# Moving the first row maxima, the spills and the loads of a float32 attention and gated-FFN kernel, with new round orders

## The chip, the cores and the metric

The kernel runs on one core of a Trainium2 chip. The metric is the device time of one execution in microseconds (us), the median over several executions. One more execution is taken with the hardware profiler; its trace is what the views below show.

## The reference

For x of 2048 tokens by 448 features the reference computes an attention block with 16 heads of 28 features, a gated feed-forward block with 1792 hidden features, and mixes the two by a sigmoid gate per token:

```
qkv = x @ wqkv                       # 448 -> 3 x 16 heads x 28
p   = softmax(q k^T / sqrt(28))      # per head, 2048 x 2048
a   = (p v).reshape(S, 448) @ wo
h   = relu(x @ W_gate) * (x @ W_up)  # 448 -> 1792
b   = h @ W_down                     # 1792 -> 448
g   = sigmoid((x * gate_w).sum(-1))
out = g * a + (1 - g) * b
```

All of it is float32.

## The kernel before, in words

**Precision.** A float32 operand is split into a high and a low float32r part, high on ScalarE (`act_high`), low as operand minus high on VectorE (`low`) or on GpSimd (`pool_low`). A product over 448 features takes eleven matmuls (the list `TERMS`): 3 1/2 chunks of 128 features, high by high, high by low and low by high, some of them packed in one matmul.

**First phase (L511 to L606).** The program loads x in four blocks of 512 tokens (`X[tb]`, two parts each), projects part of q and k (`qk`, twelve units), writes them to HBM as `qk_d`, then projects v (`vproj`, sixteen units). The last nineteen of these units stand in the list `mixed`, counted by `n`: n = 0 to 2 are q and k units, n = 3 to 18 the v units, eleven matmuls each. At given values of n the loop also issues loads (`load_k`, `load_q`, `load_w`), splits of weights, and the spills of X to HBM (`spill_x`, table `spills`; part `(tb, r)` is written to `x_d`). From unit `first` on it strews `smax` among the matmuls of a unit: two matmuls of a head's q with its k (`sm`) into a pair of PSUM banks and one VectorE maximum over 1024 values (L259). `MAXIMA` of these are done in the first phase. When all of head 0 are done (20 of them), `smax_end` transposes them on TensorE (`mt`), and two small DMAs of `mh` (L272) write them as two more rows into the tile of q (`Q0`), so that later score matmuls subtract them. EARLY puts the first eight score units of head 0 (`s`) among the last v units. The scores of token block j = 3 (`s_0_3`, `s_2_3` and so on) do not use the `mh` rows; `s_0_0` is the first that does.

**Rounds.** After that come 32 rounds, two for each head (a round is one half of the keys). Each is a string, R0 to R31, that gives the order of the work, a letter for each step: `s` a score unit (two matmuls, one ScalarE evacuation), `m` an `smax` of a later head, `x` one matmul of a projection that is spread over the rounds (first the rest of q and k, 176 matmuls, L669; then the units of gate and up, 22 matmuls each, L661), `b`, `A` running minima and the row correction on VectorE for the chunks that go uncorrected ("raw"), `g` a subtraction on GpSimd (L340), `e`, `E` exponentials on ScalarE over 1024 or 2048 columns, `P`, `Q` the two halves of probabilities times v (32 matmuls of 32 columns each, `po`, L720), `n` `smax_end`, `w` the split of a gate/up weight, and `N`, `c`, `f`, `D` small steps. The order of instructions on every engine is the order of this text: no scheduler changes it. An engine that waits holds back all that stands behind it in its queue.

X[0] is a single pair of tiles. When the last unit of a token block has used a chunk of it, `next_x` (L656) has SyncE load the next block's chunk from `x_d`; the next unit starts with the same chunk nine matmuls later. At the start of an even round SyncE gets the loads of k, and at its ninth `s` those of q, of the head after next.

**Last phase (L899 on).** What is left of gate and up is done between the down projections (`down`, L955). Four output projections (`wout`, L914) follow for each block of tokens; `split_o` (L903 to L907) splits the normalised attention output into `on0`, `on1`, in two halves of 1024 columns: the high part on ScalarE, the low part on GpSimd.

**Queues.** Loads and most stores are issued by SyncE in the order of the program; the stores of the first phase (`qk_d`, `v_d`, `x_d`) by GpSimd.

Of the kernel before, what the change touches and what calls it, by code (L numbers as in the profile page):

```python
# [72 lines left out]
R12 = "sxxsxxgxxbsxwxbwsbxxxsxxxsxxxssxxAxxswsxgExxmxwmsxxxmxxxsmxsgxxmxmxxEsbxsgxxsEbebPAmmeQ"

R13 = "sxxmsbsxxgxxxsxxsxxxbbxsxxxsxsxAsmnxgsxxxxsxmEsxxxexxmxmxxxsmxxgmxxxEmxNcsgxxsxbxsebbAePfeQ"

R14 = "mxsxxsssxxxxbbxxxbsxxxxsxxxsgsxxxxsxxAsmsxxsgxmxxxesmgxemxexxmsexexsbxPebgesemxmbxxAxQ"

R15 = "ssxsgxxsgxbxbxbxxxAgxsxxxsxxxsxsxsxsxxmexNxxxmxsmnxsxxsmeemxxxexxxxxmssxxcxsPxbbbeAegmefmxxeQ"

R16 = "smsxxbxgsxsbxxbxsxxexxsgxxxxxAsxxxsxxsmxsxexmxsmxexxmxsxxggEmxxxmsexxmxxxssxbesbbPeAQ"

R17 = "mxsmnxsggxsxxsxxxxbxxbbAxesxxxxssxxsxxxsxsmxxxsxxemxexmxsxxmxxsxxmxxexxNgmxgcEssbxxbsePebAfQ"

R18 = "smxxgsbsxxbxxgxxsxxxxbxesxxAsxesxxgxsxxxxxxmxxsmxxsmgxsxxsmsxeexxmmesePbsexxmexxxbsbAQ"

R19 = "ssxxsNxbsxxxbxxxxxgxsxgsbxAxxxssxxssxxxgmxxsxmsxmnxxsmxxxmxxmEsexbcxxgxxxsesEPxbxbAefemxmxQ"

R20 = "smgsxxsbxxxgsxxexbxsxxxbmxxsxxsAsxsxxxxxssmxxxgsxmesxmxexmxxxxmxmeEgxxxxssexxsbPebQbA"

R21 = "smsxxsxbxbxsxxxsxgbxxsAxxxgsxssxxxxmsxxxsmsnxxsxmmxxesxebxNxxmxxsxbxxgsxxxxbcgmxxxeAmePEefeQ"

R22 = "sxmsxxsxxbxggsbxxsxxxxbsxxxsAssxxxxmxsxxgsxsEmgxmxxsxmExxxxmxxsemxbsPbxeemsxexxxbxQA"

R23 = "sNmxsxxsxbxsgxxgxxbsxxxxexxbxAsxxssxxmxxxnsxsxxgxsmsxxmxemsxExmcxxxxsxsbxbsbPmxegeexAxxexfmQ"

R24 = "gsmsxxsxsbbxxExxxxxsbgxxmxAgxxxxsxssxxsxsxxxxmxsxmxsxsxmxxxmxExsxbssbPgExxbAemxmeQx"

R25 = "smsxsxbbxsxxbsxnxxsxxsssxxxgAxxsgexxmmNxcsgxexxxmxgsxsxxxmsExxxbxmxsxxxExxmxbsebefAPQxxmxxx"

R26 = "smsxxxsbxxxbsxxxsbxxsxxsgmsxsxgsxxAsxsxmxsmgmmexexxgsExbxxmxxxsxxxxsPbbEexexAxxxxxmQ"

R27 = "smsxxbsxxxxxsxbxsNxbxnsxxgxxsgssxxxxAxsxmexsxmxxcxsxmxgfxsxmxxxmegsxxexbsexxxsxExmPebbAmxexQ"

R28 = "smxmsxxxgxssxxxxxxxbexsxbsxbxxxssxsAxxsgxmxxxsxmsxmxxsxmmxexgmgxExexsxexxxsxsbbbxeexxxxPQA"

R29 = "sxxxxgssbngxbsxbAxxxxExxxxxxsxxsxxxxxssgsxsxxsxxsxNsxxxxxsxxxEcsxgxExbebsxxxxbexfAxxxPQxx"
# [24 lines left out]
def gated_mix_kernel(ctx, tc, x, wq, wo, wgu, wd, out):  # L132
# [43 lines left out]
    def pool_low(dst, src, high):  # L176
        nc.gpsimd.tensor_tensor(dst, src, f32(high), op=OP.subtract)
# [39 lines left out]
    def load_k(h):  # L217
        a = rows_kq(h)[0]
        k = qk_d[a:a + DH].rearrange("d r t -> (d r) t")
        for a in (0, 2 * DH):  # L220
            nc.sync.dma_start(f32(K[h % 3])[a:a + 2 * DH], k)
# [174 lines left out]
    with tc.tile_pool(name="qkv", bufs=1) as pa:  # L396
        W = pa.tile([P, 7, VO + VC], F32R, name="W")

        def load_w(c):
            c0, c1 = c * 2 * GD, (c + 1) * 2 * GD if c < G + 1 else 2 * D + VC  # L400
            wr = pa.tile([P, 4, 2 * GD + 2], F32, name=f"wr_{c0}", tag="wr", bufs=2)[:, :, :c1 - c0]
            if c > 0:
                nc.sync.dma_start(wr, wq[:, :, c0:c1])
# [162 lines left out]
        mixed += [(vproj, tb, t) for tb in range(NB - 1, -1, -1) for t in range(4)]
        spills = {2 + 2 * k: (NB - 1 - k // 2, k % 2) for k in range(2 * NB)}
        m, first, ahead = 0, 4, MAXIMA
        for n, (f, *a) in enumerate(mixed):
# [12 lines left out]
            if n == 8:  # L582
                split_w(*w3, pool_low)
            if n == 10:
                QS.append(last_q("Q2"))
                for i, j in ((GD, 12), (GD + 12, 4)):
                    nc.sync.dma_start(f32(QS[2])[i:i + j].rearrange("p j t -> p (j t)"), Q[1][GD + 2:GD + 2 + j].bitcast(F32))
# [463 lines left out]
```

## Time and profile before

| | |
|---|---|
| median of 3 runs | 1205.58 us (1205.16 to 1208.12) |
| profiled execution | 1207.77 us |
| its span in the trace | 1206.0 us |
| TensorE busy | 1184.7 us (98%) |
| VectorE, ScalarE, GpSimd busy | 75%, 73%, 62% |
| first phase and round 0 | 0 to 128.98 us |
| rounds 1 to 31 | 128.98 to 1015.33 us |
| last phase | 1015.33 to 1206.0 us |

A group of instructions in the profile reads: line, engine, operation, output<-inputs, shapes, count | busy us, mean ns of one | idle time just before, and what ended it. PE is TensorE, PEld its weight loads, DVE VectorE, ACT ScalarE, POOL GpSimd, SP SyncE. Matmuls overlap in the records: the mean of a 512-column matmul is some 400 ns, while starts in a dense stretch are 233 ns apart. A table by stretches gives for each one its length and the busy us (with the count) of each engine, then the granted TensorE clock (1.00 is full), the share of the DMA engines, and GB/s.

### The profile page before, as it was taken

The numbers are of one execution on the slowest core, as the hardware profiler recorded it, in microseconds if no ns is written. First come the engines' busy times: TensorE is split into PE (matmuls) and PEld (weight loads), VectorE is DVE, ScalarE is ACT, GpSimd is POOL, SyncE is SP. The second block draws the span as 40 slices with busy tenths as digits, with TensorE's granted clock in tenths as the row PEclk, the third lists the DMA queues.
The fourth block names the chain that finished last, engine by engine and source line by source line (L and its number), as shares of the span: only waits on it lengthen the run. The fifth ranks groups of instructions, "written<-read, shape, count | busy, mean of one in ns | idle before, by whom it ended". The sixth has DMA issues, their size and how long they took to land.

```text
span 1206.0 us, 16979 instructions
## 1 busy us (share of the span) xinstructions
PE 1184.7 (98%) x6183; PEld 825.1 (68%) x6183; DVE 899.1 (75%) x1171; ACT 881.2 (73%) x1023; POOL 746.6 (62%) x325
## 2 busy tenths in 40 slices
PE   9799999999999999999999999999999999999998
PEld 6688666666666666666666666666666666899998
DVE  5486889888888889889888988888888553643342
ACT  5227888998989888888888888888787887422121
POOL 5232766897889778767776777667666777531020
PEclk9899999999999999999999999999999999999999
DMA  9983574736363654344346344342724335743342
GB/s 304 327 310 117 172 237 160 217 129 185 122 191 124 207 166 141 103 134 118 119 134 215 104 132 125 112 139 98 217 89 139 102 104 160 232 135 112 110 140 81
DMA packets 70656, 188.87 MB, mean 157 GB/s; under 512 B 13946, under 2 KB 20546, under 8 KB 65666
## 3 DMA queue, kind: packets, MB, share of 16 engines
q1 hardware_dynamic: 65756, 167.78, 44.9%
q0 software_dynamic: 4384, 19.53, 4.3%
q8 instruction: 49, 0.80, 0.3%
q10 hardware_dynamic: 432, 0.46, 0.1%
q14 instruction: 35, 0.29, 0.1%
HBM read 126.96 MB, written 60.96 MB: 156 GB/s over the span
## 4 chain that ended last, share of the span: by engine, by line
PE 86%; DMA 4%; DVE 3%; ACT 3%; issue 1%; SPq 1%; POOL 1%; DVEq 0%; ACTq 0%; POOLq 0%
PE gu L661 21%; PE po L720 19%; PE s L361 18%; PE sm L255 10%; PE acc L955 9%; PE qk L669 3%; PE wo L914 3%; PE v L500 3%; DVE r L311 2%; ACT P L367 1%; DMA X<-x_d 1%; DMA Q<-qk_d 1%; DMA or<-o_d 1%; ACT P L365 1%; DMA wor<-wo_d 1%
## 5 line engine op out<-in xcount | busy, mean ns | idle before, releaser
L340 POOL TENSOR_TENSOR P<-P,rm 128x2048 f32<-128x2048 f32 x102 | 470.7, 4632 | 127.8 <-DVE rm L334 111.2
L661 PE MATMUL gu<-X,wg 128*128 128x512 f32 x1232 | 364.3, 397 | 3.2 <-DMA X<-x_d 3.2
L259 DVE TENSOR_REDUCE mx<-sm 128x1 f32<-128x1024 f32 x256 | 306.1, 1217 | 62.5 <-PE sm L255 61.2
L361 PE MATMUL s<-Q,K 128*128 128x512 f32 x1024 | 319.5, 402 | 1.6 <-DVE r L311 0.3
L661 PEld LDWEIGHTS gu<-X,wg 128*128 128x128 f32 x1232 | 229.9, 188 | 73.4 <-issue 8.7
L361 PEld LDWEIGHTS s<-Q,K 128*128 128x128 f32 x1024 | 182.6, 188 | 80.5 <-DVE r L311 12.5
L367 ACT ACTIVATE P<-s 128x1024 f32<-128x1024 f32 x204 | 203.8, 1028 | 45.8 <-PE s L361 43.5
L720 PE MATMUL po<-P,V 128*32 128x512 f32 x1640 | 230.6, 595 | 0.0
L365 ACT ACTIVATE P<-s 128x1024 f32<-128x1024 f32 x206 | 202.4, 1031 | 19.3 <-PE s L361 17.2
L351 ACT ACTIVATE P<-P 128x1024 f32<-128x1024 f32 (+1 forms) x158 | 202.6, 1312 | 0.9 <-POOL P L340 0.5
L255 PE MATMUL sm<-K,Q 128*128 128x512 f32 x520 | 163.8, 401 | 8.3 <-DMA Q<-qk_d 8.1
L311 DVE SCALAR_TENSOR_TENSOR r<-s,r 128x1024 f32<-128x1024 f32 x124 | 151.7, 1223 | 25.7 <-ACT P L367 15.1
L720 PE MATMUL po<-V 128*32 128x512 f32 x408 | 137.1, 595 | 0.0
L720 PEld LDWEIGHTS po<-P,V 128*32 128x32 f32 x1640 | 61.2, 110 | 110.5 <-issue 106.6
L340 POOL TENSOR_TENSOR V<-V,rm 128x2048 f32<-128x2048 f32 x24 | 111.1, 4631 | 31.3 <-DVE rm L334 29.9
L255 PEld LDWEIGHTS sm<-K,Q 128*128 128x128 f32 x520 | 94.3, 189 | 40.9 <-POOL K L578 8.5
L168 ACT ACTIVATE hh<-hr 128x512 fp32r<-128x512 f32 x52 | 32.8, 631 | 114.9 <-PE acc L955 114.9
L174 DVE TENSOR_TENSOR hh<-hr,hh 128x512 fp32r<-128x512 f32 x52 | 48.6, 942 | 80.3 <-ACT hh L168 80.3
L955 PE MATMUL acc<-WD,hh 128*128 128x448 f32 x480 | 100.0, 368 | 0.0
L955 PEld LDWEIGHTS acc<-WD,hh 128*128 128x128 f32 x480 | 91.1, 190 | 7.3
L311 DVE SCALAR_TENSOR_TENSOR r<-s,P 128x1024 f32<-128x1024 f32 x50 | 61.2, 1223 | 26.6 <-ACT P L367 26.1
L326 DVE TRANSPOSE_TENSOR_REDUCE mn<-r 128x32 f32<-128x1024 f32 x63 | 77.8, 1235 | 1.3
(91 smaller groups left out, 1139.2 us busy)
## 6 DMA issues: line engine op xcount, KB each, us to landing
wg<-ws_d SPq DMA_DIRECT2D x42, 896.0 KB
K<-qk_d SPq DMA_DIRECT2D x32, 448.0 KB
Q<-qk_d SPq DMA_DIRECT2D x64, 224.0 KB
X<-x_d SPq DMA_DIRECT2D x56, 256.0 KB
h_d<-h SPq DMA_DIRECT2D x56, 256.0 KB
hr<-h_d SPq DMA_DIRECT2D x52, 256.0 KB
ws_d<-wg SPq DMA_DIRECT2D x14, 896.0 KB
x_d<-X POOLq DMA_DIRECT2D x8, 1024.0 KB, 8.9
```

The costliest lines, as they stand in the source:

```text
L255: nc.tensor.matmul(ps[:, c, :], Q[h][:, u * P:(u + 1) * P], K[h % 3][:, k0:k0 + TB], start=True, stop=True)
L259: nc.vector.tensor_reduce(to, ps, axis=AX.XY, op=OP.max)
L311: nc.vector.scalar_tensor_tensor(r, ps, -1.0, before, op0=OP.mult, op1=OP.min)
L326: nc.vector.tensor_reduce(MN[:, 1:3], R2.pop((v, j)).rearrange("p a (b r) -> p a b r", r=32), axis=AX.X, op=OP.min, apply_transpose=True)
L340: nc.gpsimd.tensor_tensor(QUAD[q], QUAD[q], m, op=OP.subtract)
L351: nc.scalar.activation(q, q, AF.Exp, scale=-SCALE)
L361: nc.tensor.matmul(ps[:, c], K[h % 3][:, k * P:(k + 1) * P], Q[h][:, j * TB:(j + 1) * TB], start=True, stop=True)
L365: nc.scalar.activation(dst, ps, AF.Exp, scale=SCALE)
L367: nc.scalar.activation(dst, ps, AF.Copy, scale=-1.0)
L661: nc.tensor.matmul(ps, WS[i][:, s, a], xf(i // NF, b), start=(n == 0), stop=(n == NT - 1))
L720: nc.tensor.matmul(po[32 * j:32 * j + 32], V[:, h // 4 % 2, k, h % 4], AT.pop((v, k, j)), start=(k == k0), stop=(k == k0 + NK // 2 - 1))
L955: nc.tensor.matmul(ACC[i // NF][t][:, :D], HH[i][:, a, t * P:(t + 1) * P], wd_high_low(f, b), start=(f == 0 and n == 0), stop=(f == NF - 1 ...
```

## The change

It has five parts.

1. `MAXIMA` goes from 36 to 32, and `first` from 4 to 6: the strewn maxima begin two v units later, and four of them move into round 0, whose string now has four `m`.
2. Loads and spills of the first phase: `load_w(3)` goes from ahead of the first head's k and q to behind them (n = 1), k and q of the second head from n = 0 to n = 2, the third weight load from 2 to 3, k of the third head from 6 to 7, the split of that weight from 6 to 10, and the third q tile (`Q2`) from 10 to 13. The eight spills of X, at n = 2, 4, ... 16 before, go to 7, 8, 9, 10, 11, 12, 14, 16, in another order.
3. The strings of all rounds are new. Rounds 19 to 28 now use R11 to R18 over again. A period of eight rounds has 308 `x`, which is fourteen units, one token block. The number of `x`: rounds 0 to 10 as before (44 in rounds 0 to 3, then 40 and 43 in turn); rounds 11 to 28 have 40 (odd) and 37 (even) in place of 43 and 40 (45 in round 28); rounds 29 to 31 have 54 each in place of 50, 47, 50. The sum is 1320 in place of 1364: 59 fewer in rounds 11 to 28, 15 more in rounds 29 to 31, and 44, two units of gate and up, in the last phase.
4. `w` stands in rounds 3 to 10 only (3 to 12 before).
5. For the first token block `split_o` takes the low part on VectorE.

```
-MAXIMA = 36
+MAXIMA = 32
...
-R0 = "xxxsbxxxbxxbxxxxssxxxxsxxAsxxsxxxxsxsxxsxgxxxxxsebxxsxxxxxesxxbxxgbePAeQ"
+R0 = "xxbbsssxxxxsxbxmxxxsxxxxxssxxxxsxAxsxxxxxxmxxxxxgsbsxexxebxxsxxxgmxbxxmePAeQ"
...
-R11 = "xsmxxxgsswxbxwxxxwxxsxxxxxxbsbmsxxsmnsxxssxAxxssxgmxsExxgmmmxxxsEwxxxgNbxxxmxEsbcexexsxbAPfQxx"
+R11 = "sxsxbsxxbgxxxsxxxxsbxxxgsxxsxxssxAxsmgnsxxmsxmNxsxmxEExxxmmsxxxxbxscxxseexxbgefebxxxmAPQ"
...
 ROUNDS = [
     R0, R1, R2, R3, R4, R5, R6, R7,
     R8, R9, R10, R11, R12, R13, R14, R15,
-    R16, R17, R18, R19, R20, R21, R22, R23,
-    R24, R25, R26, R27, R28, R29, R30, R31,
+    R16, R17, R18, R11, R12, R13, R14, R15,
+    R16, R17, R18, R11, R12, R29, R30, R31,
 ]
...
         split_w(*w4)
-        w3 = load_w(3)
         load_k(0)
         load_q(0)
...
-        spills = {2 + 2 * k: (NB - 1 - k // 2, k % 2) for k in range(2 * NB)}
-        m, first, ahead = 0, 4, MAXIMA
+        spills = dict(zip((7, 8, 9, 10, 11, 12, 14, 16), ((3, 0), (2, 0), (2, 1), (1, 0), (3, 1), (1, 1), (0, 0), (0, 1))))
+        m, first, ahead = 0, 6, MAXIMA
         for n, (f, *a) in enumerate(mixed):
             if n == 0:
                 split_w(*w5)
+            if n == 1:
+                w3 = load_w(3)
+            if n == 2:
                 load_k(1)
                 load_q(1)
-            if n == 2:
+            if n == 3:
                 w2 = load_w(2)
...
-            if n == 6:
+            if n == 7:
                 load_k(2)
-                split_w(*w2, pool_low)
             if n == 8:
                 split_w(*w3, pool_low)
             if n == 10:
+                split_w(*w2, pool_low)
+            if n == 13:
                 QS.append(last_q("Q2"))
...
-        pool_low(ON[tb][1][:, c], OR[tb][:, c], ON[tb][0][:, c])
+        (pool_low if tb else low)(ON[tb][1][:, c], OR[tb][:, c], ON[tb][0][:, c])
```

How the instructions stand on two engines at the places that matter. First TensorE, from the first v unit (`v_0`, n = 3) on; `sm` is a maximum's pair of matmuls. Before:

```order
L500 MATMUL v_0_445<-W,X_3_121 128x450 x7
L500 MATMUL v_0_445<-W,X_3_122 128x450 x4
L500 MATMUL v_1_461<-W,X_3_121 128x450 x4
L255 MATMUL sm_468<-K_104,Q_107 128x512 x2
L500 MATMUL v_1_461<-W,X_3_121 128x450 x3
L500 MATMUL v_1_461<-W,X_3_122 128x450
```

and now:

```order
L480 MATMUL v_0_444<-W,X_3_121 128x450 x7
L480 MATMUL v_0_444<-W,X_3_122 128x450 x4
L480 MATMUL v_1_459<-W,X_3_121 128x450 x7
L480 MATMUL v_1_459<-W,X_3_122 128x450 x4
L480 MATMUL v_2_473<-W,X_3_121 128x450 x7
L480 MATMUL v_2_473<-W,X_3_122 128x450 x4
L480 MATMUL v_3_487<-W,X_3_121 128x450 x4
L235 MATMUL sm_494<-K_104,Q_107 128x512 x2
```

The first maximum stands behind 37 matmuls of v in place of 15.

Next SyncE's queue around the first head's k and q (`K_104`, `Q_107`; the second head's are `K_105`, `Q_108`, and `wr` are raw weights). Before:

```order
L403 DMA wr_373<-wq 128x4x224
L221 DMA K_104<-qk_d 56x2048 x2
L230 DMA Q_107<-qk_d 28x2048 x4
L221 DMA K_105<-qk_d 56x2048 x2
L230 DMA Q_108<-qk_d 28x2048 x4
```

and now:

```order
L201 DMA K_104<-qk_d 56x2048 x2
L210 DMA Q_107<-qk_d 28x2048 x4
L383 DMA wr_401<-wq 128x4x224
L201 DMA K_105<-qk_d 56x2048 x2
L210 DMA Q_108<-qk_d 28x2048 x4
```

One weight load moved from ahead of the first q to behind it; the second head's loads still follow directly in this queue. GpSimd's queue, not shown, had the first spill of X among its stores of `qk_d`, and now has it behind them all.

Last, SyncE's queue a little later: the third q tile (`Q_625`, now `Q_684`), the first raw gate/up weights (`wgr`), and the `mh` rows for head 0. Before:

```order
L587 DMA Q_625<-Q_108 12x2048
L587 DMA Q_625<-Q_108 4x2048
L230 DMA Q_625<-qk_d 28x2048 x4
L272 DMA Q_107<-mh_711 1x12x128 x2
L385 DMA wgr_716<-wgu 128x1024
L385 DMA wgr_718<-wgu 128x1024
```

and now:

```order
L570 DMA Q_684<-Q_108 12x2048
L570 DMA Q_684<-Q_108 4x2048
L210 DMA Q_684<-qk_d 28x2048 x4
L365 DMA wgr_691<-wgu 128x1024
L365 DMA wgr_693<-wgu 128x1024
L252 DMA Q_107<-mh_755 1x12x128 x2
```

The `mh` rows now stand behind the two weight loads, and the Q2 loads ahead of both are issued at unit 13 in place of unit 10, in a tile that the spilled part (3, 1) of X leaves free.

More of the change, by code (lines that the diff above doesn't have):

```diff
@@ L73 @@
[L73 to L107, printed above, removed]
@@ L109 @@
-R30 = "sxxsbxssxbxgbgxxsxxsxxAExgxxxxxxsxxssxxxxxxxgsxxsssxxExxxxsExxxxxxxsebsbPxxxbAxeDDxQ"
-R31 = "xsxxxxgxxgxsxbxsbsxxbxxsxxxxAsxxssxxexxxgxxxxxgxxxessxNxxxxxseDxxxxexxxExcxeexPsxDfQ"
+R0 = "xxbbsssxxxxsxbxmxxxsxxxxxssxxxxsxAxsxxxxxxmxxxxxgsbsxexxebxxsxxxgmxbxxmePAeQ"
+R1 = "nsmsxxsgbxbxsxxxgxsxxbxsxxxsxsxxxssAxxmxxsxmsxxmxxxmxgmgExexxxxsxmsxsxxexbsxxbEcxxebmxPeNAfQ"
+R2 = "smsxggbxxsxsxxxsxxbxsbxxxxxssxxxsxxAxggsmxxsxsxExxxmmsxxxmxxxsxsxexbxxxxbxsmebxeeAexPemmQ"
+R3 = "gsmNsxsbxsxwxsbbExxxAxxssmxxwxgxxsxxxxxxxwxmEmcsnxxxgxgxxsxxxsxmxsxxxxmmxfExsxxmxxxssbbsbeePAQw"
@@ new lines @@
+R4 = "smsxxsbxxxwwxxsxxbsgbxxxsxxmsxsxxsxsxsAxmxwxsxxsmsgxgxxxExxbxmxxeexmmxxgxsPbxEesxembwQAx"
+R5 = "NsxxsxxssbgxxxbxxxxwbxxxxsmnxsxsmAsxxswgsxsxxEmxxmxxxxsxxsxmxxEmxxmgsbxexxxxsxxmbegxscbefPeAwwQ"
+R6 = "smsxxxxgxbwssgxxxxxxxsxxxbbxxwemxAssxxxssxsxxmxxsxxsmsxgxexmmsexgbexxxxxsEbemPsewmxwQbxAx"
+R7 = "wssxxbxxsNbxxsbxxxxxgwxsxxxsxmsxsxxxxAsxsgxsxxmnxmxxxesxwsgexmmxxsxbsxxxxcexxsbbAexxmPEgmexfemQw"
+R8 = "smsxgxxswsxxxbxsxwbxbxxsxAxsxxssxgxsmxxgsxxsxmgxxExmxsEmxxmxxwxsxmsbPExxexbmxsxbAxexwQx"
@@ new lines @@
+R9 = "ssxsxbxsxxbxbxxxNxxsxsxAxgxggssxxxxsxsxmmExxsxxmxxsxxmwxmxsxxwmxwexsxnesEbbcsPxgmbxeAxxxxfxemQw"
+R10 = "sxswxxsgxxxxxbsxwxsxgbwbxsxxAxxesxgxxxxssxxmsxxsxxmsxexmxsxEmxxmxxsxgxbwmEmPEmsxbsxxQbA"
+R11 = "sxsxbsxxbgxxxsxxxxsbxxxgsxxsxxssAxsmgnsxxmsxmNxsmxmEExxxxmmsxxxxbxscxxseexxbgefebxxxmAPQ"
+R12 = "sxgssbxgxxxxsbxxxsbxxxxsxxsxssxxsAxmxxsxxsmEmxxsxmxxgxxExmxsgxbsbxsPbExxeAxemmmQ"
+R13 = "sxxsxgxbssxbexbNxxxgxxxsxxxsxxsxxxAsxxsxmnxcsxxsmexxxgxgsmsexxmxxmsxsbxbxxsexEbxeAPmfmemQ"
+R14 = "xsmsxxsbxxxgsexxxxbbAsxxxxsxxsssxxsxxmxgxxgxxsmxsxemxxmsExmxxxxssmPgEbebmsbAxexQx"
@@ new lines @@
+R15 = "sNmsxxsxsxxxbgxbxsbxxnxsxxsxsxsxAxxxsmsExgxmxxmxscxsxexmxxxmgxmxxmxxxEsxxbxsxsbePgefebAQ"
+R16 = "sxmsxgxsxxsxxbexbxsxxgxbmAxxxsxsgsxxxxssxmxxsxxsxemxmxgsExxmxxxssmEebPbsmexQxbAxx"
+R17 = "smsxxbxsxxsxbNxbxxsxgxsxxxssxxAxxnxssmxxexxxmxsmxgxxmesxxsxmgxxEmExgmsxxcxxbxsexbsfbePAQ"
+R18 = "xgsmsxbxsxxxbxxsbxxsxxAsxxxsgsxxssxxxxmsxexmxxxsxxgsmxxemxexxmxesmgEePsebmxxsbbxAQ"
+R29 = "sxxsxxssxxxbxxxxgxxEbgxxsxxbxxsxsxsxxNxxxxsAxxsxssnxsxxxcxsxxxxxxggExxExxsbxxxxexbxxsbeAfPQxx"
+R30 = "DsxxsxgxsxxxxxsxbxsbxxExxxbxxxxssxAxxxxgxsgxsxxsxxxsssxxxxxxxsxEsxxgxExxbexxxxxsebDxxxPbQxA"
@@ L113 @@
+R31 = "xxsxxsbxxxxxxsxxbxssxbxxxxxsxxsxxxsxsxxsxxxAxxgxEgxxxxexxxxxgxgsexxNDxexxexxxexDexcsfxPQ"
 ROUNDS = [
```

10 lines of the change are left out of this document (removed).

## The prediction, made before the changed kernel ran

> **What bounds the kernel now.** I read the page's list of engines first.
>
> ```profile
> PE 1184.7 (98%) x6183; PEld 825.1 (68%) x6183; DVE 899.1 (75%) x1171; ACT 881.2 (73%) x1023; POOL 746.6 (62%) x325
> ```
>
> TensorE is busy for 98% of the span, and the change leaves its matmuls as they are and only moves them. So time can be won only where it waits or runs below its pace. The waits of PE, longest first:
>
> ```profile
> PE sm L255 <- DMA Q<-qk_d: 8.1, 1, 8.1
> PE gu L661 <- DMA X<-x_d: 3.2, 2, 2.0
> PE wo L914 <- POOL on L177: 2.9, 1, 2.9
> ```
>
> Columns: us in all, times, longest. These three are nearly all of its idle time, and the change touches each. A wait can cost more than its length, which the tables by stretches show (length, busy us of PE, PEld, DVE, ACT, POOL, then the granted clock, DMA share, GB/s):
>
> ```profile
> 41.50:44.00 2.50, 0.08 (x1) 0.00 (x0) 0.00 (x0) 0.00 (x0) 0.00 (x0) 1.00 0.96 270
> 44.00:46.00 2.00, 0.00 (x0) 0.00 (x0) 0.00 (x0) 0.00 (x0) 0.00 (x0) 0.54 0.90 346
> 54.00:55.00 1.00, 1.00 (x5) 0.85 (x5) 0.55 (x2) 0.61 (x2) 0.00 (x0) 0.81 0.92 328
> 852.00:856.00 4.00, 1.99 (x9) 1.34 (x9) 1.93 (x3) 1.76 (x3) 1.87 (x1) 1.00 1.04 325
> 1052.00:1055.00 3.00, 0.15 (x2) 0.09 (x1) 3.00 (x2) 0.00 (x0) 3.00 (x3) 0.92 0.60 175
> 1055.00:1058.00 3.00, 3.00 (x9) 2.69 (x10) 0.40 (x1) 0.00 (x0) 2.50 (x2) 0.52 0.42 137
> ```
>
> In the 8.1 us wait the clock falls to a half about 2.5 us in (44.1), and comes back at 54.4 (0.81 of the last stretch is 0.38 us at a half). After the 2.9 us wait it is 0.52 for 3 us. The 2.0 us wait inside 852 to 856 left it at 1.00. So a wait of 2 us costs its length, one of 3 us or more costs a few us at half pace besides.
>
> For the rounds I need what the matmuls must take. Starts in dense stretches, and a pair of P and Q:
>
> ```profile
> 999.00 3.20 PE L661 MATMUL gu<-X,wg 128*128 128x512 f32 x13
> 1002.03 1.09 PE L361 MATMUL s<-Q,K 128*128 128x512 f32 x4
> 122.04 7.00 PE po L720 x64
> ```
>
> (1002.03 - 999.00) / 13 = 0.233 us for 512 columns; P and Q take 7.0. A round with 16 `s` and 8 `m` has 48 matmuls, 11.2 us, so 18.2 with P and Q, and 0.233 for each `x`: 27.5 with 40, 28.2 with 43, 26.8 with 37. Measured rounds, cut where the last `po` of a round ends (5 to 11; 19 to 25; 26; 29 to 31):
>
> ```profile
> 244.13:445.85 201.72, 200.84 (x1083) 127.73 (x1079) 171.52 (x222) 182.97 (x210) 171.03 (x78) 1.00 0.52 160
> 646.59:844.87 198.28, 198.10 (x1077) 127.28 (x1073) 174.63 (x232) 171.89 (x181) 139.97 (x44) 1.00 0.39 119
> 844.87:877.53 32.66, 30.46 (x163) 19.00 (x159) 26.10 (x34) 23.87 (x24) 22.06 (x6) 1.00 0.68 209
> 935.49:1015.33 79.84, 79.20 (x432) 49.60 (x428) 40.32 (x63) 71.90 (x77) 64.47 (x23) 1.00 0.33 101
> ```
>
> The first needs 7 x 18.2 + 292 x 0.233 = 195.4 (rounds 5, 7, 9, 11 have 43), so it loses 6.3 us or 0.9 a round; there ScalarE is busy 183.0 of 201.7, 91%. The second needs the same and loses 2.9, 0.4 a round, at 87%. Round 26 loses 32.7 - 27.5 = 5.2. The last three need 88 x 0.233 + 21 + 147 x 0.233 = 75.8 and lose 4.0. Busy PE in these rows hides most of that: a matmul's record stretches over a short wait.
>
> **The change, part by part.** I start at the first maximum.
>
> ```profile
> 33.52 0.54 SPq L403 DMA_DIRECT2D wr<-wq  x1
> 36.37 0.79 SPq L221 DMA_DIRECT2D K<-qk_d  x2
> 37.20 3.45 SPq L230 DMA_DIRECT2D Q<-qk_d  x4
> 38.20 0.65 POOL L464 DMA_DIRECT2D x_d<-X  x1
> 39.93 9.62 DMA Q<-qk_d
> 38.34 3.23 PE L500 MATMUL v<-W,X 128*128 128x450 f32 x15
> ```
>
> The first five rows are the way of head 0's q: last issue about 39.9, landed 49.55, with the DMA engines 0.9 to 1.0 busy. PE does 15 matmuls of v from 38.34, at (3.23 - 0.38) / 14 = 0.204 us, and stops at 41.5. Lost: 8.1 us, and half of the 4.7 us from 49.7 to 54.4, 2.35. Together 10.45.
>
> Now 37 matmuls of v stand ahead of the first maximum: 38.34 + 37 x 0.204 = 45.9. If q lands as before, 3.7 us are left. It should land earlier: the weight load (0.46 MB) is no longer ahead of it in SyncE's queue and the 1.05 MB spill no longer beside it, 1.5 MB of the some 4 MB that 12.5 us move at 320 GB/s. Fully given to q that is 4.7 us, not at all 0. Part of the weight load had landed when q was issued, and a spill of GpSimd's shared the engines with its own stores ahead of it, so I take 1.7: landed at 47.9, 2.0 us of wait, and by the row at 852 no fall of the clock. **Gain 8.4**; bounds 4.4 (3.7 us and the same 2.35 at half pace) and 10.4.
>
> The next suspect is behind it, since the spills start at unit 7 in place of 2:
>
> ```profile
> SPq L587 <- DMA x_d<-X: 7.4, 1, 7.4
> DMA to landing us min/median/max: 6.1/8.9/14.1
> 61.30 1.48 SPq L587 DMA_DIRECT2D Q<-Q  x2
> 62.83 3.09 SPq L230 DMA_DIRECT2D Q<-qk_d  x4
> 84.08 1.32 SPq L385 DMA_DIRECT2D wgr<-wgu  x2
> 81.64 0.27 PE L267 MATMUL mt<-ident,m 128*12 128x128 f32 x1
> 99.35 0.69 PE L361 MATMUL s<-Q,K 128*128 128x512 f32 x2
> ```
>
> SyncE waited 7.4 us for a spill (second row: how long spills take) before it could load Q2. Now that spill, part (3, 1), goes at unit 11. A unit of v is 2.25 us with 1.15 for its 2.46 maxima, so unit 10 is done at 38.3 + 3 x 2.25 + 2.0 + 5 x 3.4 = 64.1, and the spill is issued near 66, landed at 75 to 80. Behind it SyncE issues Q2 (1.5 + 3.1 us), `wgr` (1.3), and only then `mh`: 81 to 86. TensorE has `mt` near 78.5 and the first score that needs `mh`, `s_0_0`, 28 v and 18 wide matmuls later, 9.9 us (17.7 before, the last two rows), at 88.4. Two transfers of a few KB then have 2 to 7 us to land. I charge **1.0**; bounds 0, and 4 if they land behind the 2.1 MB of Q2 and `wgr` at half of the engines. The DMA: Bandwidth & Descriptors page of the Trainium skill (Queues, rings and completion order) says that each DMA engine takes the descriptors of one queue in their order and goes round between queues; by that rule `mh` would come behind all of it, and the charge would be 4.
>
> The reload of X at a block's end:
>
> ```profile
> 421.36 4.94 SPq L656 DMA_DIRECT2D X<-x_d  x8
> 632.79 3.15 SPq L230 DMA_DIRECT2D Q<-qk_d  x4
> 641.90 0.73 PE L661 MATMUL gu<-X,wg 128*128 128x512 f32 x2 [1.23 <-DMA X<-x_d]
> 846.47 0.92 SPq L221 DMA_DIRECT2D K<-qk_d  x2
> 854.65 0.73 PE L661 MATMUL gu<-X,wg 128*128 128x512 f32 x2 [2.01 <-DMA X<-x_d]
> ```
>
> Of three block ends among the gate/up units two wait, in rounds 18 and 26, where SyncE has loads of q between the chunks, or of k just ahead. The third, in round 11 (first row), did not, with 22 wide matmuls (5.1 us) from the free chunk to its next use. Now all three fall at the 19th `x` of R11's string, in rounds 11, 19 and 27, which are odd and have no such loads; 24 wide matmuls, 5.6 us, lie between. The waits are worth 3.2, and round 26 lost 5.2 - 0.4 = 4.8 with its 2.0, so 2.8 more behind it, where ScalarE has four evacuations to catch up. **Gain 5**, bounds 3.2 and 6.
>
> The output projection's low part:
>
> ```profile
> 1048.96 1.04 ACT L168 ACTIVATE on<-or 128x1024 fp32r<-128x1024 f32 x1
> 1050.51 1.60 POOL L177 TENSOR_TENSOR WD<-wdr,WD 128x448 fp32r<-128x448 f32 x1
> 1052.07 2.78 POOL L177 TENSOR_TENSOR on<-or,on 128x1024 fp32r<-128x1024 f32 x1
> L174 DVE TENSOR_TENSOR X<-ox,X 128x1024 fp32r<-128x1024 f32 x2 | 2.4, 1224 | 3.5 <-ACT X L168 3.5
> ```
>
> ScalarE had the second half's high part at 1050.0; GpSimd began its low part 2 us later, behind that of a weight, and took 2.8. VectorE takes 1.2 for the same shape, somewhat more if its records stretch as in the row at 1052 (two in 3 us): the wait of 2.85 is then all but gone. With the wait go the 1.45 us that the 0.52 over 3 us lost: 4.3 in all. The two units moved here (44 matmuls, 10.3 us) come before these projections and would cover the wait too. **Gain 4.1**, bounds 2.9 and 4.3. The TensorE: Matmul & The Clock Gate page of the Trainium skill (Part 1) lets the clock fall after an idle window of about 3.4 us. By that figure 2.85 us would have cost no clock and the gain would be 2.9; the row at 1055 shows that it did.
>
> The rounds. Rounds 11 to 28 lose 59 `x`, 13.8 us; 3.5 come back in rounds 29 to 31, 10.3 in the last phase, where TensorE is the bound as well: nothing, if the shorter rounds do get shorter. There ScalarE has 171.9 / 7 = 24.6 us a round, VectorE 24.9, now against 27.15 of matmuls: 89 to 91% busy, between the 87% at which a round loses 0.4 and the 91% at which it loses 0.9. **Cost 4.5**, 18 rounds at 0.25; bounds 0 and 9. In rounds 29 to 31 some of the 15 more matmuls fill the 4.0 us lost there: **gain 1**, bounds 0 and 3.5. The new strings of rounds 1 to 10 I take at nothing, by 3 either way, since their load stays.
>
> The four moved maxima cost TensorE nothing, and around round 0
>
> ```profile
> 95.00:150.00 55.00, 55.00 (x272) 39.91 (x271) 42.39 (x55) 44.09 (x55) 29.23 (x10) 1.00 0.38 130
> ```
>
> VectorE (42.4 of 55 us) has the 4 x 1.2 us to spare; were it full, 4.9 us. The later weight splits wait for nothing as long as q's loads run ahead.
>
> Sum: -8.4 + 1.0 - 5 - 4.1 + 4.5 - 1 = -13.0 on the profiled execution's 1207.77 us (span 1206.0): 1194.8. The median of the runs lies 2.2 lower, so **1192.6**.
>
> **Rivals.**
>
> *The `mh` rows come late.* For it speaks the 7.4 us wait above, against it that 9.9 us suffice if spills land at the median. TensorE waits 4 us, and the clock falls for some 2.3 more: 5.3 over my charge, 1198.
>
> *Q lands no earlier.* The stores that GpSimd still queues may be what held it. Gain 4.4 in place of 8.4: 1196.6.
>
> *The shorter rounds stay as long as rounds 19 to 25*, 198.28 / 7 = 28.3 us each, because the chain of score, evacuation and running minimum sets them and not TensorE. 18 x (28.3 - 27.15 - 0.4) = 13.5 in place of 4.5: 1201.6. Against it: rounds with 40 `x` already run shorter than those with 43 by about the difference.
>
> *They become as slow as rounds 5 to 11, and slower than before.* If ScalarE's order blocks PSUM at 90% as it did there, a round takes 201.72 / 7 = 28.8: 18 x 1.65 = 29.7 less the 7.2 that 0.4 each stand for, 22.5 in place of 4.5, so 1210.6. The point from which it decides is a loss of some 1.5 us a round in rounds 11 to 28. Against it: those rounds also carried the weight splits (`w`), which the new ones don't.
>
> **How the numbers follow.** My forecast 0.62, `mh` late 0.11, q no earlier 0.10, rounds unshortened 0.10, rounds slower 0.07. A change under 0.3% (3.6 us) can't be told from none here. The first three cases are faster; the fourth lies on that edge and I split it; some doubt about terms that no row shows goes from faster to the others: 0.85, 0.08, 0.07. The forecast's own range is 1185 to 1199; with the other cases it is 1184 to 1203, which leaves the last case out.
>
> **What would show it.** The first `sm` of the changed trace starts near 48, with a wait of some 2 us on q and a clock of 1.00 after it. No PE wait on X, none on `on`, and 1.00 in the clock around the first `wo`. Round 0 ends near 121 (128.98 now). An even and an odd round of 11 to 28 take 55.6 us together. From the last `po` to the end 10.3 - 4.1 us more than the 190.7 of now. A PE wait on `mh` at the first `s_0_0`, or rounds of 28 us and more, would make me wrong.

## The result, and the profile after

| | before | after |
|---|---|---|
| median (lowest to highest) | 1205.16 us (1201.16 to 1208.12, 5 runs) | 1216.88 us (1214.88 to 1217.86, 5 runs) |
| span of the profiled execution | 1206.0 us | 1215.0 us |
| first phase and round 0 | 128.98 | 136.93 |
| rounds 1 to 31 | 886.35 | 871.72 |
| last phase | 190.67 | 206.35 |

The change makes the kernel slower: the ratio is 1.0097, with a 95% interval of 1.0072 to 1.0122. The prediction was 1192.6 us, 1184 to 1203, and faster with 0.85, so it was wrong in sign and in size. The rounds gained what was forecast and more (14.6 us). The first phase with round 0 lost 8.0 us where it should have gained about 8, and the last phase grew by 15.7 where it should have grown by 6.2. Of the variants below, one execution of the first (Q2 late) took 4135.85 us; its other nine took 1201.9 to 1206.23, and its ratio goes by these nine.

The list of engines of the changed kernel, and its longest PE waits (us in all, times, longest):

```profile
PE 1188.5 (98%) x6183; PEld 824.6 (68%) x6183; DVE 896.1 (74%) x1173; ACT 878.8 (72%) x1018; POOL 741.5 (61%) x323
```

```profile
PE s L341 <- DMA Q<-mh: 10.9, 1, 10.9
PE gu L644 <- DMA wg<-ws_d: 5.8, 1, 5.8
PE sm L235 <- DMA Q<-qk_d: 2.1, 1, 2.1
```

The share of TensorE, 98%, is that of before and tells nothing. The waits tell it: X and `on` are gone from the list, the wait on q is down to 2.1 us, and two new ones stand above it. The table by stretches (length, busy us of PE, PEld, DVE, ACT, POOL, granted clock, DMA share, GB/s) around the three waits:

```profile
46.00:51.00 5.00, 2.86 (x9) 2.37 (x9) 1.23 (x1) 0.00 (x0) 1.80 (x1) 0.78 0.99 308
51.00:56.00 5.00, 5.00 (x22) 4.36 (x22) 3.68 (x3) 0.95 (x3) 1.60 (x3) 0.87 0.95 232
96.00:101.00 5.00, 0.00 (x0) 0.00 (x0) 0.00 (x0) 0.00 (x0) 0.00 (x0) 0.50 0.72 189
101.00:106.00 5.00, 3.85 (x10) 3.27 (x11) 0.64 (x1) 1.02 (x1) 0.00 (x0) 0.50 0.00 1
106.00:111.00 5.00, 5.00 (x23) 4.27 (x22) 2.59 (x3) 2.55 (x4) 0.00 (x0) 0.91 0.00 0
1026.00:1030.00 4.00, 2.51 (x6) 2.05 (x7) 0.00 (x0) 0.00 (x0) 0.89 (x1) 0.50 1.08 318
1030.00:1035.00 5.00, 5.00 (x19) 3.97 (x19) 0.00 (x0) 0.11 (x1) 0.39 (x1) 0.81 0.57 220
```

After each wait a stretch runs at half the clock. Behind q it is (0.22 x 5 + 0.13 x 5) x 2 = 3.5 us at a half, 1.75 lost; behind `mh` 102.15 to 106 and 0.9 more, 2.4 lost; behind the gate/up weights 1027.49 to 1030 and 1.9 more, 2.2 lost.

Where the `mh` rows were so long can be read upwards from TensorE's wait through the queues (the trace's instructions in order of time, merged: start, us, engine, line, operation, and the idle time before it with what ended it):

```profile
48.23 0.60 SPq L383 DMA_DIRECT2D wr<-wq  x1
...
69.97 1.23 ACT L148 ACTIVATE wb<-wr 128x576 fp32r<-128x576 f32 x4 [6.88 <-DMA wr<-wq]
...
70.79 2.50 POOL L157 TENSOR_TENSOR wb<-wr,wb 128x576 fp32r<-128x576 f32 x4 [10.47 <-ACT wb L148]
...
74.87 1.59 POOL L444 DMA_DIRECT2D x_d<-X  x3
...
81.99 2.21 SPq L570 DMA_DIRECT2D Q<-Q  x2
84.25 7.93 SPq L210 DMA_DIRECT2D Q<-qk_d  x4
92.23 1.47 SPq L365 DMA_DIRECT2D wgr<-wgu  x2
93.81 1.63 SPq L252 DMA_DIRECT2D Q<-mh  x2
...
102.15 1.19 PE L341 MATMUL s<-Q,K 128*128 128x512 f32 x2 [10.93 <-DMA Q<-mh]
```

The third weight load (`wr`) is issued at 48.23, about when it was in the kernel before (48.06). ScalarE reaches the split of it (n = 10) and waits 6.9 us; GpSimd has the low part of that split, and behind it in its own queue the spills of n = 10 to 16. It waits 10.5 us and issues the spill that Q2 needs, (3, 1), at 74.9. In the kernel before GpSimd stood even longer at this split, but that spill (n = 4) was ahead of it in the queue:

```profile
49.35 0.54 POOL L464 DMA_DIRECT2D x_d<-X  x1
63.22 2.49 POOL L177 TENSOR_TENSOR wb<-wr,wb 128x576 fp32r<-128x576 f32 x4 [13.34 <-ACT wb L168]
```

So it is the new order that does the harm, which the second experiment below tests: the spill now stands behind the split. Around the end of GpSimd's stand the memory has little left to do:

```profile
71.00:76.00 5.00, 5.00 (x26) 4.43 (x25) 4.54 (x6) 1.79 (x8) 4.92 (x10) 1.00 0.36 146
```

SyncE's own table of waits has what this does to it:

```profile
SPq L570 <- DMA x_d<-X: 28.1, 1, 28.1
```

It stands before Q2 until that spill has landed, at 82.0, needs 10.2 us to issue Q2's six loads (4.6 before), issues `wgr`, and only at 93.8 the few KB of `mh`. They land at 102.

In the last phase it is a single load:

```profile
1008.65 10.57 PE L644 MATMUL gu<-X,wg 128*128 128x512 f32 x44
...
1019.50 0.38 SPq L629 DMA_DIRECT2D wg<-ws_d  x1
...
1027.49 7.36 PE L644 MATMUL gu<-X,wg 128*128 128x512 f32 x22 [5.83 <-DMA wg<-ws_d]
```

The weights of a gate/up unit (0.9 MB) go into one of two `wg` tiles. The two units at the head of the phase free theirs at 1014 and 1019, but the load of the next stands in SyncE's queue behind the phase's other loads, goes out at 1019.50 and takes 7.9 us.

Last the rounds, cut as before (all of 1 to 31; 11 to 18; 19 to 25; 26; 29 to 31):

```profile
136.93:1008.65 871.72, 870.56 (x4711) 555.25 (x4707) 735.44 (x973) 769.25 (x835) 659.06 (x232) 1.00 0.47 143
425.49:648.62 223.13, 222.99 (x1212) 141.71 (x1208) 196.90 (x259) 194.23 (x203) 159.45 (x48) 1.00 0.45 134
648.62:844.53 195.91, 195.75 (x1063) 124.35 (x1059) 174.03 (x231) 170.35 (x178) 140.92 (x44) 1.00 0.40 122
844.53:872.08 27.55, 27.55 (x153) 17.28 (x149) 23.23 (x29) 23.75 (x25) 18.45 (x4) 1.00 0.58 164
928.76:1008.65 79.89, 79.89 (x447) 52.68 (x443) 42.13 (x66) 71.00 (x77) 62.81 (x23) 1.00 0.37 115
```

Rounds 19 to 25 have 7 x 18.2 + (4 x 40 + 3 x 37) x 0.233 = 190.5 us of matmuls and take 195.9: they lose 0.77 each, where rounds of 40 and 43 lost 0.4.

### The profile page after: what moved, and what is told of

Same layout as the page of the kernel before. It is cut to its first block, busy times and chain, and to the rows that moved or that the text cites. A ratio compares the mean times of both kernels' runs of the same rounds, so it can differ in the third digit from the quotient of the medians.

```text
span 1215.0 us, 16951 instructions
## 1 busy us (share of the span) xinstructions
PE 1188.5 (98%) x6183; PEld 824.6 (68%) x6183; DVE 896.1 (74%) x1173; ACT 878.8 (72%) x1018; POOL 741.5 (61%) x323
## 5 line engine op out<-in xcount | busy, mean ns | idle before, releaser
L341 PE MATMUL s<-Q,K 128*128 128x512 f32 x1024 | 320.7, 403 | 12.6 <-DMA Q<-mh 10.9
L291 DVE SCALAR_TENSOR_TENSOR r<-s,r 128x1024 f32<-128x1024 f32 x124 | 151.8, 1224 | 20.8 <-ACT P L347 10.2
L154 DVE TENSOR_TENSOR hh<-hr,hh 128x512 fp32r<-128x512 f32 x52 | 45.2, 875 | 78.2 <-ACT hh L148 78.2
## 6 DMA issues: line engine op xcount, KB each, us to landing
x_d<-X POOLq DMA_DIRECT2D x8, 1024.0 KB, 10.5
```

The lines of the kernel that those rows point to most:

```text
L291: nc.vector.scalar_tensor_tensor(r, ps, -1.0, before, op0=OP.mult, op1=OP.min)
L341: nc.tensor.matmul(ps[:, c], K[h % 3][:, k * P:(k + 1) * P], Q[h][:, j * TB:(j + 1) * TB], start=True, stop=True)
```

## The experiments

Gains below are differences of the ratios to the kernel before, times 1205 us, since its own median differed a little from set to set (1205.2 to 1206.5); a ratio carries some 2 to 3 us either way, and a gain, which is the difference of two, 3 to 4. What each theory says of `mh` and of the gate/up weights stands in the expectations.

**Q2 and the raw weights behind the `mh` rows.** On the changed kernel:

```
-            if n == 13:
+            if n == 16:
                 QS.append(last_q("Q2"))
...
-            if n == len(mixed) - 6:
+            if n == 16:
                 fetch_f(0)
```

> The changed kernel, with the loads of the third q tile (Q2) and of the first raw gate/up weights issued at unit 16 in place of 13, so behind the mh rows in SyncE's queue. Theory A, a chain of queues: TensorE's 10.9 us wait for mh at the first s_0_0 exists because SyncE stood for 28.1 us at the Q2 load, for the spill of part (3, 1). Then mh is issued right after it is ready (about 81), lands well before s_0_0 (about 91), the wait is gone and with it some 2.2 us at half clock: 13 us faster than the changed kernel, about 1204. Theory B, bytes: the DMA engines are so far behind that mh lands at about 95 or later wherever it stands: a wait of 4 us or more stays, gain at most 7 us.

Measured: 1203.9 us, ratio 0.9985 (0.9968 to 1.0002), a gain of 13.5. SyncE's queue and the PE waits of this kernel:

```profile
81.44 2.27 SPq L252 DMA_DIRECT2D Q<-mh  x2
83.81 2.75 SPq L570 DMA_DIRECT2D Q<-Q  x2
```

```profile
PE gu L644 <- DMA wg<-ws_d: 5.1, 1, 5.1
PE sm L235 <- DMA Q<-qk_d: 2.7, 1, 2.7
```

`mh` goes out 12.4 us earlier, the wait on it is gone, and round 0 ends at 124.06 in place of 136.93. So the `mh` wait and its clock are 13 us, more than the 8.0 by which the first phase and round 0 had grown.

**The split of the third weight later**, so that GpSimd doesn't stand in front of its spills; the order in SyncE's queue is kept:

```
-            if n == 10:
+            if n == 15:
                 split_w(*w2, pool_low)
```

> The changed kernel, with only the split of the third weight load (w2) at unit 15 in place of 10, so that ScalarE and GpSimd do not stand at it with four spills behind them. Theory A with this cause: spills go out from about 64 on, part (3, 1) lands near 75, Q2 is issued from 75, mh at about 85, landed by 88 to 92; the wait falls from 10.9 to 0 to 3 us, 9 to 13 us faster, 1204 to 1208. Rival C, the order of mh behind Q2 and the raw weights in SyncE's queue is the larger part: mh still lands 8 us after its issue, a wait of 4 to 6 us stays, gain 5 to 8 us. Rival D, the spills were late only because of their place in the table: gain under 3 us.

Measured: 1211.16 us, ratio 1.0041 (1.0024 to 1.0058), a gain of 6.7.

```profile
PE s L341 <- DMA Q<-mh: 4.6, 1, 4.6
```

```profile
77.59 1.48 SPq L570 DMA_DIRECT2D Q<-Q  x2
79.12 3.47 SPq L210 DMA_DIRECT2D Q<-qk_d  x4
82.64 1.01 SPq L365 DMA_DIRECT2D wgr<-wgu  x2
83.75 1.63 SPq L252 DMA_DIRECT2D Q<-mh  x2
```

The stand on GpSimd was half of it. Part (3, 1) is spilled at 66.33, where the prediction had it (near 66), and Q2 goes out at 77.59. `mh` now is issued at 83.75, which is within the 81 to 86 that the prediction had worked out, and still lands only at 93.8. So the prediction's issue time would not have saved it: the way from the issue to the landing takes 10 us there, where 2 to 7 were left.

**Only the raw weights behind `mh`:**

```
-            if n == len(mixed) - 6:
+            if n == 16:
                 fetch_f(0)
```

> The changed kernel with only the first raw gate/up weights (wgr, two loads of 0.5 MB) moved behind the mh rows; the Q2 loads stay ahead of them. It parts the wait for mh in two: the time that SyncE stands at Q2 and its four loads, and the time that mh takes to land behind the raw weights. If mh was slow because 1 MB stood ahead of it on the same queue, it lands some 2 us after its issue at about 92 to 94: a wait of 4 to 5 us in place of 10.9, 6 us faster than 1216.9. If not, it lands near 100 and the gain is under 2 us.

Measured: 1212.8 us, ratio 1.0049 (1.003 to 1.0069), a gain of 5.8.

```profile
91.28 1.62 SPq L252 DMA_DIRECT2D Q<-mh  x2
...
96.87 1.19 PE L341 MATMUL s<-Q,K 128*128 128x512 f32 x2 [5.61 <-DMA Q<-mh]
```

Issued 2.5 us earlier, landed 5.3 us earlier: the 1.05 MB of raw weights ahead of it in the same queue cost the `mh` rows about 2.8 us beside the time of their issue. The rest of the wait goes with SyncE's stand at Q2, as the first experiment shows, which put `mh` ahead of both. The DMA: Bandwidth & Descriptors page of the Trainium skill (Queues, rings and completion order), by which a DMA engine takes one queue's descriptors in their order, agrees with these two landings, 93.81 to 102.15 with the weights ahead and 91.28 to 96.87 without.

**The two moved gate/up units later in the last phase**, after the fifth and sixth down projections, where their weights have long landed:

```
-        if done + 2 + i < NB * NF:
-            todo.append((gate_up, done + 2 + i))
+        if i >= 4 and done - 2 + i < NB * NF:
+            todo.append((gate_up, done - 2 + i))
```

> The changed kernel, with the last two gate/up units of the last phase behind down projections 4 and 5 in place of 0 and 1. Theory A: the 5.8 us wait for the weights (wg) is there because only two weight tiles exist, the load for unit 54 can be issued only when unit 52 is done, and it stands behind the loads at the head of the phase; four more down projections (9.7 us) cover it. Wait gone, and some 2 to 3 us at half clock: 8 us faster than the changed kernel, about 1209. Rival: the head of the phase is bound by its loads as such, and with the units out of the way the first down projections wait for their own operands: gain under 3 us.

Measured: 1208.17 us, ratio 1.002 (1.0002 to 1.0038), a gain of 9.3. PE has no wait on `wg` any more; the one on `mh` stays, 11.0 us. So the weight load, 5.8 us with 2.2 of clock, is shown as the other part of the loss.

**Both**, the first and the last of these edits on the changed kernel:

> The first and the third of these edits together. If the two waits are separate, the gains add: 13 + 8 = 21 us faster than the changed kernel, about 1196, and so faster than the kernel before by some 9 us, near my first forecast of 1192.6. If something else takes their place (weights or spills later), 1200 to 1208.

Measured: 1196.49 us, ratio 0.9919 (0.9892 to 0.9946): the two gains add up (21.5 against 22.8), and this kernel is faster than the changed one and than the one before. Of the PE waits over 0.7 us only that on q is left, 2.2 us, beside one of 1.2 us at the very start that every version has. It takes the clock with it:

```profile
46.00:51.00 5.00, 2.92 (x9) 2.48 (x10) 1.22 (x1) 0.00 (x0) 1.80 (x1) 0.76 0.96 289
```

**The first maximum one more v unit later**, on top of both; `MAXIMA` is 34, and two `m` leave round 0:

```
-MAXIMA = 32
+MAXIMA = 34
...
-        m, first, ahead = 0, 6, MAXIMA
+        m, first, ahead = 0, 7, MAXIMA
```

> The version with both edits (e4_both, 1196.5), with the maxima from unit 7 in place of 6: 34 of them in the first phase and two in round 0. Eleven more matmuls of v (2.24 us) stand ahead of the first one, so TensorE comes to it at about 48.1, where the first q lands at 48.2. Theory: the 2.2 us wait and the half clock behind it (0.76 and 0.89 in the two stretches of 5 us from 46 on, 1.7 us) both go: 3.5 us faster, about 1193. Rival: the maxima are now closer, VectorE falls behind or mh comes late again, and the wait only moves: within 1 us of 1196.5.

Measured: 1192.74 us (1192.27 to 1193.31), ratio 0.9885 (0.9868 to 0.9902), the best version of this study, 1.15% under the kernel before.

```profile
46.00:51.00 5.00, 4.97 (x24) 4.11 (x24) 2.12 (x2) 0.89 (x3) 3.35 (x4) 1.00 0.95 286
```

No wait on q, no fall of the clock, and round 0 ends at 121.30. The 4 us gained over the last kernel fit the 2.2 of the wait and some 1.75 of clock.

**The third weight load ahead of the first k and q again**, on top of both, to see what made q land earlier:

```
+        w3 = load_w(3)
         load_k(0)
...
-            if n == 1:
-                w3 = load_w(3)
```

> The version with both edits, with one weight load (w3) back ahead of the first head's k and q, as in the kernel before. It tells what of q's earlier landing (48.2 in place of 49.6) is that load's and what the late spills'. If the load's: q lands near 49.5, the wait grows from 2.2 to 3.5 us, with its clock 1.5 to 2.5 us slower than 1196.5. If the spills': no difference, within 0.5 us.

Measured: 1196.65 us, ratio 0.9918 (0.99 to 0.9936), no difference; the first maximum starts at 48.25 (48.08 with both edits alone). So the 0.46 MB of the load did not hold q up. The prediction's other candidate, the spill that shared the engines, was not tried by itself. But the last two runs of this section keep the first phase of before, with the load and the spill where they were, and their first maxima don't start at 49.68 either:

```profile
48.09 1.19 PE L255 MATMUL sm<-K,Q 128*128 128x512 f32 x2 [7.21 <-DMA Q<-qk_d]
48.62 1.19 PE L235 MATMUL sm<-K,Q 128*128 128x512 f32 x2 [7.24 <-DMA Q<-qk_d]
```

Counted from the first matmul of v, the first maximum starts after 10.4 to 11.3 us in the three traces with the old first phase, and after 9.8 to 10.5 in the eight with the new one in which it waits. The means, 10.75 and 10.1, differ by 0.65 us, which is all that the two transfers together are shown to cost q; more than half of its earlier landing is a difference between traces.

**The low part of `on` on GpSimd again**, on top of both:

```
-        (pool_low if tb else low)(ON[tb][1][:, c], OR[tb][:, c], ON[tb][0][:, c])
+        pool_low(ON[tb][1][:, c], OR[tb][:, c], ON[tb][0][:, c])
```

> The version with both edits, with the low part of the first output projection back on GpSimd. The prediction said that the two gate/up units moved ahead of these projections cover the wait as well, so that VectorE here is worth nothing: no wait on `on`, within 1 us of 1196.5. Rival: GpSimd is still late behind the weights' low parts, a wait of 2 to 3 us returns with its half clock: 3 to 4.5 us slower, about 1200.

Measured: 1196.29 us, ratio 0.9915 (0.9895 to 0.9936), no difference. With two units moved ahead of the projections, `on` is in time on either engine: no PE wait on it, and a last phase of 198.8 us against 199.2. In this run's trace the wait on the first q is 2.26 us, and the clock did not fall:

```profile
46.00:51.00 5.00, 2.92 (x14) 2.58 (x15) 2.12 (x2) 0.29 (x1) 1.80 (x1) 1.00 0.96 290
```

A wait in round 0, 2.1 us in place of 0.7, takes most of that back.

**That part alone, on the kernel before:**

```
-        pool_low(ON[tb][1][:, c], OR[tb][:, c], ON[tb][0][:, c])
+        (pool_low if tb else low)(ON[tb][1][:, c], OR[tb][:, c], ON[tb][0][:, c])
```

> The kernel before with one part of the change alone: the low part of the first output projection on VectorE. The prediction's term for it: the 2.85 us wait and the 1.45 us of half clock behind it go, 4 us faster than before, about 1201. Rival: the wait was not GpSimd's to keep (ScalarE had the high part only 1 us before TensorE came), and 1 us or more of it stays: gain under 3 us.

Measured: 1205.46 us against 1206.2, ratio 0.9988 (0.9971 to 1.0005): not the 4 us. Yet only 0.6 us of the wait is left and the clock does not fall, as this kernel's waits and stretches show:

```profile
PE wo L914 <- DVE on L174: 0.6, 1, 0.6
```

```profile
1050.00:1055.00 5.00, 4.40 (x22) 3.69 (x21) 3.25 (x4) 0.65 (x2) 2.04 (x1) 1.00 0.36 116
1080.00:1110.00 30.00, 30.00 (x147) 27.25 (x146) 9.65 (x12) 7.08 (x11) 4.82 (x2) 1.00 0.38 112
```

The same stretch of the kernel before, where nothing is edited either:

```profile
1080.00:1110.00 30.00, 30.00 (x150) 27.81 (x149) 10.83 (x14) 6.95 (x11) 5.11 (x2) 1.00 0.37 106
```

147 matmuls in 30 us against 150, at the same granted clock. In these two traces the gain goes there: the 9 + 2 + 12 matmuls around the wait took 9.14 us before (1050.07 to 1059.21) and 5.58 now (1048.50 to 1054.08), 3.6 gained; from there to the end 146.8 us before and 149.7 now, 2.9 given back by a pace 2% slower. Whether the slow pace comes with the edit or with the single execution is not shown; executions of the kernel before lie anywhere from 1201.78 to 1210.58 us in this set. More on the two paces stands further down.

**The new strings alone, on the kernel before**, with its own first phase, `MAXIMA` 32, and the two units late in the last phase:

```
-MAXIMA = 36
+MAXIMA = 32
...
-    R16, R17, R18, R19, R20, R21, R22, R23,
-    R24, R25, R26, R27, R28, R29, R30, R31,
+    R16, R17, R18, R11, R12, R13, R14, R15,
+    R16, R17, R18, R11, R12, R29, R30, R31,
...
-        if done + 2 + i < NB * NF:
-            todo.append((gate_up, done + 2 + i))
+        if i >= 4 and done - 2 + i < NB * NF:
+            todo.append((gate_up, done - 2 + i))
```

The strings R0 to R31 are those of the change.

> The kernel before with the new round strings (and 32 maxima in the first phase, which they need, from unit 4 on), its own first phase and its low part on GpSimd, and the two moved gate/up units behind down projections 4 and 5. Theory: rounds 1 to 31 take the 871.7 us that they take in the changed kernel in place of 886.4, wherever they start (14.6 us), the last phase 8.5 us more than before as in e4_both, round 0 as before: 6 us faster, about 1199. Rival: the strings need the new first phase, and rounds 1 to 3 or the start lose what they win: no faster than 1203.

Measured: 1201.83 us, ratio 0.997 (0.9954 to 0.9986), 3.6 us faster where some 6 were expected. The rounds of this kernel:

```profile
129.30:1001.14 871.84, 870.64 (x4712) 555.10 (x4708) 735.53 (x973) 769.22 (x835) 659.09 (x232) 1.00 0.47 144
```

871.84 us is within 0.2 of the changed kernel's 871.72, though it starts 7.6 us earlier. So the strings bring their 14.5 us with either first phase, and the last phase takes 9.2 back (199.9 against 190.67).

## Why the prediction was wrong, point by point

On the spans the forecast was -13.0 us and +9.0 was measured. Two terms make 20.3 of these 22: the charge for `mh` (12.3 too small) and the last phase's "nothing" (8.0 too small).

**The first q: nearly right.** The first maximum starts at 48.30 with a wait of 2.14 us (forecast near 48, 2 us). "By the row at 852 no fall of the clock" failed: it cost 1.75 us, so the gain was 6.6 and not 8.4. The credit for the earlier landing does not hold: the load and the spill that were to make q land 1.7 us sooner are worth some 0.65 us together. More than half of the 1.4 us by which q landed earlier than in the trace before is a difference that traces of one and the same first phase show too, so that the wait came out at 2 us was in part luck. The 22 matmuls more ahead of the first maximum are what shortened the wait.

**"I charge 1.0" for `mh`: the mechanism right, the size wrong, and this alone is 12.3 us.** The wait and its clock took 10.9 + 2.4. The rival that named it had 4 us of wait and a chance of 0.11; it went wrong in two terms. "The spill is issued near 66": it was 74.9. The sum for it counted TensorE's units alone and came out right where GpSimd was free (66.33 with the split later). What it left out is that the spill now stands behind a weight split in GpSimd's queue, and the prediction had said of these that "the later weight splits wait for nothing as long as q's loads run ahead": this one waited, 6.9 us on ScalarE and 10.5 on GpSimd. And "two transfers of a few KB then have 2 to 7 us to land", with 4 us as the upper price: with the issue where the prediction had it they took 10 (the run with the split at n = 15). Its sentence on the DMA queue's order, which would have made the charge 4, had the right direction and was still short.

**X and the rounds: right.** No PE wait on X is left. Round 26 takes 27.55 us for 37 `x`, 26.8 of matmuls: it loses 0.7 in place of 5.2. Rounds 11 to 28 pay 0.3 to 0.4 more each (4.5 forecast), far from the 1.65 of the rival that was to be slower than before; so that rival is excluded. The unshortened rounds are too, though rounds 19 to 25 became only 2.4 us shorter for 4.9 us of matmuls fewer. In rounds 29 to 31, 162 `x` take 79.89 us where 79.3 are needed; 3.4 of the 4.0 lost there came back, and the prediction had 1. All rounds together gained 14.6 us against a forecast of 11.8 (13.8 + 5 - 3.5 - 4.5 + 1).

**"Nothing, if the shorter rounds do get shorter" for the last phase: wrong by 8.0 us.** The 44 matmuls were costed by their pace, but not the weights that they read: what was moved is a unit, and a unit brings a load of 0.9 MB into a ring of two tiles, whose issue stands behind what SyncE already has at the head of that phase. No rival spoke of it.

**`on` on VectorE: worth nothing here.** 4.1 us was booked on one wait that the same paragraph said the two moved units would also cover. On the changed kernel that is what they do (GpSimd again: no difference). On the kernel before, the part by itself removes all but 0.6 us of the wait and all of its clock, as forecast, and its runs show 1.4 us (-0.6 to 3.5): in its trace a slower pace behind it gives most of the gain back.

Summed up on the spans: -6.6 for q, +13.3 for `mh`, -14.6 for the rounds, +10.3 for the moved matmuls, +8.0 for their weights, -4.3 for the `on` wait that is gone, and some +1 for a slower pace of the last 50 us (further down), which is 7; measured are 9.0. Of the 2 that are missing 1.3 lie in the first phase and round 0, and nothing in the trace names them. Without the two waits the changed kernel is at 1196.49, 3.9 us over the forecast: 1.75 of clock behind q, and by estimate some 2 of pace in the last phase (2% of the 107 us from 1041 to 1148).

## What to carry to other kernels

A moved step drags its queue neighbours: before a split or a load is put later, list what stands behind it on each engine that takes part, the DMAs that a compute engine issues above all, and follow each to the one that waits for it; here a spill came to stand behind a split that waited, GpSimd stood 10.5 us, SyncE issued Q2 4.4 us and `mh` 10.1 us later than with the split moved out of the way, and TensorE's wait was 10.9 us in place of 4.6. A transfer of a few KB that someone waits for is priced by the megabytes ahead of it in its queue, so it goes ahead of bulk loads in the program. And when work is moved to another phase, its operands' loads are moved as well: check the ring of tiles they land in and the place of their issue there, and count a wait that two edits remove only once.

## What was not expected of the hardware

**Two paces of matmul at one granted clock.** The 448-column matmuls of the last phase run at either of two paces. Of the changed kernel, the same 44 matmuls of two output projections, and a short wait between them:

```profile
1123.34 9.08 PE L897 MATMUL wo<-WO,on 128*128 128x448 f32 x44
...
1162.33 5.12 PE L938 MATMUL acc<-WD,hh 128*128 128x448 f32 x22 [0.31 <-DVE hh L154]
1167.29 9.26 PE L897 MATMUL wo<-WO,on 128*128 128x448 f32 x44
```

And of the best version, the other way round:

```profile
1099.24 9.26 PE L897 MATMUL wo<-WO,on 128*128 128x448 f32 x44
...
1138.96 5.09 PE L938 MATMUL acc<-WD,hh 128*128 128x448 f32 x22 [0.29 <-DVE hh L154]
1143.89 9.08 PE L897 MATMUL wo<-WO,on 128*128 128x448 f32 x44
```

9.08 or 9.26 us, 2% apart, held for some 100 us and more and changed at a wait of 0.3 us, in either direction. In six other traces it changes between the same two projections (in five to the quick pace, in one to the slow one) with no wait listed there. In the kernel before the quick pace lasted to the end, its 2.85 us wait notwithstanding; with the low part on VectorE a wait of 0.6 us left the slow one to the end. The first output projections are quick in four of the twelve traces (before, changed, Q2 late, raw weights late), and each of these had run at half the clock shortly before, in the same phase; of the other eight only the one with the split later had. That is a lead and no cause: no run aimed at it. It is up to 3 us in this last phase, as much as many an edit there is worth.

**A wait of about 2 us may or may not cost the clock.** With waits of 2.1 to 2.7 us on the first q it fell in the traces of the changed kernel and of five of its variants (Q2 late, the raw weights late, the gate/up units late, both, and both with the weight load first). It did not with 2.26 us there in the run with GpSimd's `on`, nor with 2.13 us in round 0 of the same run, 2.04 us on q in the run with the split later, and 2.01 us in round 26 of before. The TensorE: Matmul & The Clock Gate page of the Trainium skill (Part 1) has the clock fall after an idle window of about 3.4 us; these rows show it fall after less, and that the length alone doesn't decide. The cause of the difference stays open, so such a wait should be given both prices, 0 and 1.75 us.

**The memory idle in a phase that it bounds.** The DMA share was 0.36 between 71 and 76 us, in the middle of 0.9 to 1.0, because the engine that issues the spills stood at a weight; with the split later it stays at 0.99 or more from 66 to 76. And SyncE needed 10.2 us to issue six loads that took it 4.6 before and 5.0 with the split later; four spills of 1 MB went out just ahead of the 10.2. In the six other traces with these four spills between 72 and 77 the six loads took 7.9 to 10.8 us, and 5.9 in the one where they went out from 66 to 70 (both with the weight load first). That the spills slowed the issue is still a guess; no run tried it by itself.

**VectorE beside GpSimd.** The second of two equal subtractions took 2.18 us in the run with `on` on VectorE alone, the first 1.23. GpSimd was at work through the whole of the second (its records from 1048.59 to 1052.04, the subtraction from 1048.86 to 1051.04), and through some half of the first. The longer one left the wait of 0.6 us there; that GpSimd is the cause is only argued.
